# First loads of an attention and expert kernel spread over two queues in another order, with the function table loaded between them

## The chip, the core and the metric

The kernel runs on one core of a Trainium2 chip. The metric is the device time of one execution in microseconds. Five engines work side by side, each through its own list of instructions in order: PE (TensorE: matrix products, with weight loads shown apart as PEld), DVE (VectorE), ACT (ScalarE), POOL (GpSimd) and SP (SyncE). DMAs are issued by instructions on SP and ACT here, and each of the two feeds a queue of its own; an instruction that issues a DMA stands in its engine's list like any other.

## What is computed

The reference, cut to what matters:

```
scores = scale * np.matmul(q, k.transpose(0, 1, 3, 2))        # q, k, v: (2, 8, 576, 64)
kth = np.partition(scores, -top_k, axis=-1)[..., -top_k:-top_k + 1]     # top_k = 32
scores = np.where(scores >= kth, scores, -1000000000.0)
attn = np.exp(scores - np.max(scores, axis=-1, keepdims=True))
attn = attn / (np.sum(attn, axis=-1, keepdims=True) + 1e-09)
attn_out = np.matmul(attn, v)
...
x = _moe_ref(x, ...)       # each row to its one best of 8 experts, limited capacity
return _moe2_ref(x, ...)   # the same without a limit
```

In an expert layer a row goes through `relu(x @ w1[e]) @ w2[e]` and is scaled by its gate weight.

## The kernel before, in words

Attention comes first. The two batches of eight heads are cut into eight units of two heads, and each unit has nine tiles of 128 query rows (four for each head, and one that holds the last 64 rows of both), so 72 tiles. For a tile PE makes the scores of 128 rows against 576 keys, ACT copies them out of PE's accumulators (L478), DVE finds the 32 largest of each row with a chain of folds, maxima and replacements (L505 to L525), POOL and ACT form what lies below the limit (L597, L594), PE turns that (L603, L604), ACT takes the exponential and PE multiplies with v (L624). The two expert layers follow.

The opening is written by hand in `attention()` and in `begin()`. A product with full accuracy is had by splitting k and q into a rounded part and a rest: `part_of` has ACT write the rounded part (L712), DVE subtract it (L717) and POOL copy k (L714). `whole` has PE turn the parts (L285) so that the head's 64 numbers lie on partitions, and ACT or DVE copies them out (L723, L725). `scores(0, 0)` follows once the last 64 rows have been turned too (`put_tails`, L299).

Ahead of `begin()` stand the first instructions of three lists. PE has 17 products of constants into `xb` (`spin`, L124), which keep it at work until data come. SP and ACT issue the loads of unit 0: `load(0, ("k",))` on SP (L261 the first 512 rows of both heads in one DMA of 256 KB, L262 the last 64 rows, 32 KB) and `load(0, ("q",), nc.scalar)` on ACT (L259 twice, 128 KB for each head, and L262). ACT then loads its function table for the exponential (L796) by a small activation `warm`. SP goes on with q of unit 1, v of unit 0 (`vraw`, L253 and L254), k of unit 1, the gate weights and the rest. ACT's next instruction after `warm` is L712 on the first head of k.

Each DMA of SP and ACT adds to a semaphore when it has landed, and there are eight such semaphores, DMAHW0 to DMAHW7, which the build deals out in turn to these DMAs. A DMA that is given a semaphore already dealt out carries a wait for that semaphore's earlier DMA, and the wait stands in the list of the engine that issues it.

Of the kernel before, what the change touches and what calls it, by code (L numbers as in the profile page):

```python
# [10 lines left out]
F32 = mybir.dt.float32  # L11
# [4 lines left out]
AF = mybir.ActivationFunctionType  # L16
# [38 lines left out]
def attn_moe_moe_kernel(ctx, tc, q, k, v, g1, w11, w12, capacity, g2, w21, w22, out):  # L55
    nc = tc.nc
    B, H, S, D = q.shape
# [4 lines left out]
    NC = (S + 127) // 128  # L62
    TAIL = S - (NC - 1) * 128
# [7 lines left out]
    with tc.manual_schedule():  # L71
# [12 lines left out]
        coef = consts.tile([128, 3], F32)  # L84
# [107 lines left out]
    def attention():  # L192
# [4 lines left out]
        M = NC - 1  # L197
# [4 lines left out]
        with tc.tile_pool(name="ald", bufs=2) as ld, tc.tile_pool(name="awk", bufs=2) as wk, \  # L202
                tc.tile_pool(name="aps", bufs=1, space=PS) as ps, tc.manual_schedule():
            st = {}
            held_t = []
            for i in range(2):
                qt = wk.tile([128, 2, 192], F32R, name=f"qtail{i}", bufs=1)
                nc.gpsimd.memset(qt.bitcast(F32), 0.0)
                xl = wk.tile([128, NC, 2, XW], F32, name=f"xl{i}", bufs=1)
                vT = wk.tile([128, NC, 128], F32, name=f"vT{i}", bufs=1)  # L210
# [3 lines left out]
            shifted, under, vx = [], [], []  # L214
# [18 lines left out]
            xo = xb[:, :6 * XW].rearrange("p (g h w) -> p g h w", h=2, w=XW)  # L233
            zero = blank
            pend = []

            def load(u, what=("k", "q", "v"), eng=None):
                b, p = divmod(u, HP)
                z = st.setdefault(u, {"vT": held_t[u % 2][0], "xl": held_t[u % 2][1], "qtail": held_t[u % 2][2],
                                      "v": vx[u % 4]})  # L240
                dma = (eng or nc.sync).dma_start
                for nm in what:
                    s_ = {"k": k, "q": q, "v": v, "w": v}[nm][b, 2 * p:2 * p + 2]
                    if nm == "v":
                        if "vw" not in z:
                            load(u, ("w",))
                        for hh in range(2):
                            dma(z["v"][:, :M, hh, :D], s_[hh, :M * 128, :].rearrange("(s c) d -> s c d", s=128))
                        dma(z["v"][:TAIL, M, :, :D], s_[:, M * 128:, :].rearrange("h s d -> s h d"))
                    elif nm == "w":  # L250
                        t = z["vw"] = ld.tile([128, NC, 2, D], F32, name="vraw", bufs=2)
                        for hh in range(2):
                            dma(t[:, :M, hh], s_[hh, :M * 128, :].rearrange("(s c) d -> s c d", s=128))  # L253
                        dma(t[:TAIL, M], s_[:, M * 128:, :].rearrange("h s d -> s h d"))  # L254
                    else:
                        t = ld.tile([128, 2, NC, D], F32, name=nm + "raw", bufs=2)
                        if nm == "q":
                            for hh in range(2):
                                dma(t[:, hh, :M], s_[hh, :M * 128, :].rearrange("(c s) d -> s c d", s=128))  # L259
                        else:  # L260
                            dma(t[:, :, :M], s_[:, :M * 128, :].rearrange("h (s c) d -> s h c d", s=128))  # L261
                        dma(t[:TAIL, :, M], s_[:, M * 128:, :].rearrange("h s d -> s h d"))  # L262
                        z[nm] = t.rearrange("s h c d -> s c h d")
# [426 lines left out]
            def spin(n, o):  # L690
                for _ in range(n):
                    idle_product(o)
# [97 lines left out]
            seq = [(u, t) for u in range(NU) for t in order[u]]  # L790
            pairs = {}
            spin(17, xb[:, :256])
            load(0, ("k",))
            load(0, ("q",), nc.scalar)
            warm = wk.tile([128, 1], F32, name="warm", bufs=1)
            nc.scalar.activation(warm, coef[:, :1], AF.Exp)  # L796
            load(1, ("q",))
            load(0, ("w",))
            load(1, ("k",))
# [120 lines left out]
            for i in range(L - 4):  # L920
                k_, j_ = divmod(i, 2)
# [81 lines left out]
            z = st[u]  # L1003
# [13 lines left out]
            for c in range(NC):  # L1017
                w, k_ = c % 2, c // 2
# [1088 lines left out]
    rank_cuts = (0, 3, 6, 9, None)  # L2107
    w2_order = ((0, 1), (2, 3), (4, 5), (6, 7), (0, 1), (2,), (3, 4, 5, 6, 7))
    repair(attention())
    small = [ctx.enter_context(tc.tile_pool(name=f"msm{i}", bufs=1)) for i in range(2)]  # L2110
    onehot = small[0].tile([128, 128 * max(B * NC, NCOL + nov[0])], BF, name="onehot")
# [37 lines left out]
```

## Time and profile before

| what | value |
|---|---|
| median of 3 runs | 582.66 us (582.62 to 582.76) |
| the profiled execution, its own time | 583.19 us |
| its span, first to last instruction | 581.5 us |
| share of PE, DVE, ACT, POOL busy | 97%, 82%, 72%, 46% |
| mean granted clock of TensorE | 0.996 |

A busy share is time in which the engine had an instruction under way, whatever that instruction was worth: PE's spins count too. The profiled execution took 1.69 us more than its span, which lies outside the first and last instruction, and 0.53 us more than the median.

### The profile page before, as it was taken

How to read it: one execution, taken by the hardware profiler on the slowest of the kernel's cores; microseconds unless marked ns; L12 is line 12 of the kernel's file. 1: busy time of each engine (PE TensorE's matmuls, PEld its weight loads, DVE VectorE, ACT ScalarE, POOL GpSimd, SP SyncE). 2: the span in 40 equal slices, each digit the busy share in tenths (PEclk: the TensorE clock that was granted, in tenths of full speed). 3: DMA queues.
4: the chain of work that ended last, by engine and by line, in shares of the span. 5: the costliest groups of instructions: out<-in, count | busy, mean ns of one | idle time of the engine just before them, and what ended most of it. 6: DMA issues, size and time to landing. Idle time of an engine off the chain costs nothing. (4 is left out here: it accounts for less than half of the span.)

```text
span 581.5 us, 13994 instructions
## 1 busy us (share of the span) xinstructions
PE 566.0 (97%) x4786; PEld 539.2 (93%) x4786; DVE 475.5 (82%) x1588; ACT 419.4 (72%) x1040; POOL 267.1 (46%) x600
## 2 busy tenths in 40 slices
PE   8999999999999999989999999999999999999994
PEld 6799999999999999889999999998998899999993
DVE  6999999999999999868788788552588788889640
ACT  6789998999898988637687787452465677878550
POOL 8768888988898798546320111010103302220010
PEclk9999999999999999999999999999999999999998
DMA  6630513161211482055998767875777767678650
GB/s 145 143 83 2 169 46 114 45 127 43 70 48 62 70 254 77 23 196 181 349 280 282 221 227 250 287 236 198 237 253 244 278 232 260 225 249 298 211 203 14
DMA packets 85200, 100.76 MB, mean 173 GB/s; under 512 B 33957, under 2 KB 46757, under 8 KB 85120
## 3 DMA queue, kind: packets, MB, share of 16 engines
q1 hardware_dynamic: 79136, 86.69, 48.2%
q0 software_dynamic: 3728, 10.70, 5.4%
q10 hardware_dynamic: 2256, 2.39, 1.3%
q8 instruction: 40, 0.66, 0.5%
q14 instruction: 40, 0.33, 0.2%
HBM read 86.51 MB, written 13.74 MB: 172 GB/s over the span
## 5 line engine op out<-in xcount | busy, mean ns | idle before, releaser
L624 PE MATMUL xb<-vx,pT 128*128 128x73 f32 (+1 forms) x800 | 94.0, 266 | 0.2 <-ACT pT L1014 0.2
L1367 PE MATMUL pp<-xT,w1c 128*128 128x352 f32 (+4 forms) x316 | 92.4, 361 | 0.4 <-DVE xT L1323 0.4
L1288 DVE TENSOR_TENSOR w2c<-raw,w2c 128x512 fp32r<-128x512 f32 x112 | 74.5, 684 | 18.6 <-ACT w2c L1287 16.8
L624 PEld LDWEIGHTS xb<-vx,pT 128*128 128x128 f32 (+1 forms) x800 | 87.1, 181 | 2.5 <-issue 1.3
L1406 PE MATMUL pp<-hT,w2c 128*128 128x416 f32 (+4 forms) x320 | 88.7, 356 | 0.1
L1408 PE MATMUL pp<-hT,w2c 128*128 128x208 f32 (+4 forms) x320 | 77.8, 243 | 0.0
L1369 PE MATMUL pp<-xT,w1c 128*128 128x176 f32 (+4 forms) x316 | 77.0, 244 | 0.0
L1287 ACT ACTIVATE w2c<-raw 128x512 fp32r<-128x512 f32 x112 | 67.4, 624 | 8.7 <-PE pp L1408 3.7
L603 PE MATMUL pt<-ident,shifted 128*128 128x128 f32 x350 | 67.5, 278 | 0.0
L604 PE MATMUL pt<-negid,under 128*128 128x128 bf16 x350 | 63.5, 219 | 0.5 <-ACT under L594 0.5
L1288 DVE TENSOR_TENSOR w1c<-raw,w1c 128x512 fp32r<-128x512 f32 x88 | 55.9, 684 | 9.5 <-ACT w1c L1287 7.5
L1339 ACT ACTIVATE t<-pp 128x208 f32<-128x208 f32 (+4 forms) x120 | 37.6, 314 | 34.2 <-PE pp L1369 21.6
L1408 PEld LDWEIGHTS pp<-hT,w2c 128*128 128x128 f32 x320 | 61.0, 191 | 0.0
L1406 PEld LDWEIGHTS pp<-hT,w2c 128*128 128x128 f32 x320 | 60.0, 187 | 1.0 <-DVE hT L1333 0.8
L1367 PEld LDWEIGHTS pp<-xT,w1c 128*128 128x128 f32 x316 | 59.4, 188 | 1.4 <-DVE xT L1323 0.8
L1369 PEld LDWEIGHTS pp<-xT,w1c 128*128 128x128 f32 x316 | 60.4, 191 | 0.0
L1469 POOL DMA_INDIRECT out_dram<-yr,sidx x14 | 13.6, 972 | 101.1 <-ACT yr L1450 84.7
L594 ACT ACTIVATE under<-s,nb 128x576 bf16<-128x576 f32 x70 | 54.9, 786 | 1.5 <-POOL nb L586 1.3
L1792 POOL DMA_DIRECT2D y<-yr x13 | 7.6, 582 | 105.3 <-issue 45.1
L523 DVE MAX8 top<-ypair 128x8 f32<-128x160 f32 x192 | 54.7, 313 | 0.0
L597 POOL TENSOR_SCALAR shifted<-s,nb 128x576 f32<-128x576 f32 x70 | 52.3, 747 | 3.9
L603 PEld LDWEIGHTS pt<-ident,shifted 128*128 128x128 f32 x350 | 49.2, 140 | 3.6
(421 smaller groups left out, 1547.8 us busy)
## 6 DMA issues: line engine op xcount, KB each, us to landing
raw<-in_moe_w_dram SPq DMA_DIRECT2D x60, 1024.0 KB, 5.1
w1c<-in_moe_w_dram SPq DMA_DIRECT2D x8, 512.0 KB, 6.3
y<-blank SPq DMA_DIRECT2D x3, 769.5 KB
out_dram<-blank SPq DMA_DIRECT2D x3, 768.0 KB
y<-yr POOLq DMA_DIRECT2D x8, 256.5 KB
kraw<-in_k_dram SPq DMA_DIRECT2D x8, 256.0 KB, 3.4
vraw<-in_v_dram SPq DMA_DIRECT2D x16, 128.0 KB, 2.8
vx<-in_v_dram SPq DMA_DIRECT2D x16, 128.0 KB, 2.8
```

Of the source, the lines that this page charges most:

```text
L523: ops.append(lambda w=w, cur=cur: nc.vector.max(w, cur))
L594: nc.scalar.activation(under[k % 3][:, :S], s, AF.Relu, bias=nb[:, 1:2], scale=-BIG)
L597: nc.gpsimd.tensor_scalar(shifted[k % 3][:, :S], s, nb[:, 0:1], 1.0, op0=OP.add, op1=OP.mult)
L603: both = (nc.tensor.matmul(pt[:, o], shifted[k % 3][:, o], ident, is_transpose=True, start=True, stop=False), nc.tensor.matmul(pt[:, o], u ...
L604: nc.tensor.matmul(pt[:, o], under[k % 3][:, o], negid, start=False, stop=True))
L624: nc.tensor.matmul(o, pT[:, c2, cols], z["v"][:, c2, hh], start=(c2 == 0), stop=(c2 == NC - 1))
L1287: nc.scalar.activation(o[:, 0], src_, AF.Copy)
L1288: nc.vector.tensor_tensor(o[:, 1], src_, o[:, 0].bitcast(F32), op=OP.subtract)
L1367: nc.tensor.matmul(ph[:, :2 * n].rearrange("p (w n) -> p w n", w=2), w[f][:, 0, d], xT[:, d, :, :n], start=st, stop=False)
L1369: nc.tensor.matmul(ph[:, :n], w[f][:, 1, d], xT[:, d, 0, :n], start=False, stop=sp)
L1406: nc.tensor.matmul(py[:, :2 * n].rearrange("p (w n) -> p w n", w=2), w[f][:, 0, o], hT[:, f, :, :n], start=st, stop=False)
L1408: nc.tensor.matmul(py[:, :n], w[f][:, 1, o], hT[:, f, 0, :n], start=False, stop=sp)
```

## The change

Unit 0's k and q are now loaded by a function of their own, `load_first`. ACT issues one DMA (the last 64 rows of k), loads its function table and runs `warm`, and then issues a second DMA (the second head of q). SP issues k's first 512 rows, the first head of q and the last 64 rows of q. The same five DMAs move the same bytes into tiles of the same names and sizes; nothing behind them in the program is edited.

```diff
+            def load_first(then):
...
+                kt = ld.tile([128, 2, NC, D], F32, name="kraw", bufs=2)
+                qt = ld.tile([128, 2, NC, D], F32, name="qraw", bufs=2)
+                head = lambda hh: (qt[:, hh, :M], q_[hh, :M * 128, :].rearrange("(c s) d -> s c d", s=128))
+                tail = lambda t, s_: (t[:TAIL, :, M], s_[:, M * 128:, :].rearrange("h s d -> s h d"))
+                nc.sync.dma_start(kt[:, :, :M], k_[:, :M * 128, :].rearrange("h (s c) d -> s h c d", s=128))
+                nc.scalar.dma_start(*tail(kt, k_))
+                nc.sync.dma_start(*head(0))
+                then()
+                nc.sync.dma_start(*tail(qt, q_))
+                nc.scalar.dma_start(*head(1))
...
             spin(17, xb[:, :256])
-            load(0, ("k",))
-            load(0, ("q",), nc.scalar)
             warm = wk.tile([128, 1], F32, name="warm", bufs=1)
-            nc.scalar.activation(warm, coef[:, :1], AF.Exp)
+
+            def table_load():
+                nc.scalar.activation(warm, coef[:, :1], AF.Exp)
+
+            load_first(table_load)
             load(1, ("q",))
```

Lines behind the new function are 16 and then 18 higher than before. What the built programs hold at three places, with the semaphores that each instruction waits for:

The first place is the start of ACT's list. `kraw` and `qraw` are the loaded tiles, 128x4x64 is one head's first 512 rows, 64x2x64 the last 64 rows of both heads; `ks` and `qs` are the split parts. Before, and then now:

```order
L259 DMA qraw<-in_q_dram 128x4x64 x2
L262 DMA qraw<-in_q_dram 64x2x64
L796 ACT_TABLE_LOAD
L796 ACTIVATE warm<-coef 128x1 [waits DVE_49]
L712 ACTIVATE ks<-kraw 128x4x64 [waits DMAHW1_49]
L712 ACTIVATE qs<-qraw 128x4x64 [waits DMAHW0_49]
L712 ACTIVATE ks<-kraw 64x2x64 [waits DMAHW3_49]
L712 ACTIVATE qs<-qraw 64x2x64 [waits DMAHW5_49]
```

```order
L246 DMA kraw<-in_k_dram 64x2x64
L812 ACT_TABLE_LOAD
L812 ACTIVATE warm<-coef 128x1 [waits DVE_49]
L250 DMA qraw<-in_q_dram 128x4x64 [waits DMAHW7_49]
L728 ACTIVATE ks<-kraw 128x4x64 [waits DMAHW1_49]
L728 ACTIVATE qs<-qraw 128x4x64 [waits DMAHW2_49]
L728 ACTIVATE ks<-kraw 64x2x64 [waits DMAHW0_49]
L728 ACTIVATE qs<-qraw 64x2x64 [waits DMAHW3_49]
```

Two of the three DMAs have left the list, one of another tile has come in front, and the DMA of q's second head now stands between `warm` and the first split, with a wait for DMAHW7.

The second place is the start of SP's list; `vraw` is v of unit 0, and the two L259 (now L275) load q of unit 1. Before, and then now:

```order
L261 DMA kraw<-in_k_dram 128x2x256
L262 DMA kraw<-in_k_dram 64x2x64
L259 DMA qraw<-in_q_dram 128x4x64 x2
L262 DMA qraw<-in_q_dram 64x2x64
L253 DMA vraw<-in_v_dram 128x4x64 [waits DMAHW0_49]
L253 DMA vraw<-in_v_dram 128x4x64 [waits DMAHW1_49]
L254 DMA vraw<-in_v_dram 64x2x64 [waits DMAHW2_49]
```

```order
L245 DMA kraw<-in_k_dram 128x2x256
L247 DMA qraw<-in_q_dram 128x4x64
L249 DMA qraw<-in_q_dram 64x2x64
L275 DMA qraw<-in_q_dram 128x4x64 x2
L278 DMA qraw<-in_q_dram 64x2x64
L269 DMA vraw<-in_v_dram 128x4x64
L269 DMA vraw<-in_v_dram 128x4x64 [waits DMAHW0_49]
L270 DMA vraw<-in_v_dram 64x2x64 [waits DMAHW1_49]
```

SP has one DMA more ahead of v, and the first half of v is now issued without a wait; the second half waits for DMAHW0, where before the first half did.

The third place is PE's list where v of unit 0 is turned (L776 before, L792 now). Before, and then now:

```order
L285 MATMUL pg<-identr,ks 128x128 [waits Activation_49,Pool_49]
L285 MATMUL pg<-identr,ks 128x128 x3
L776 MATMUL pt<-ident,vraw 128x128 [waits DMAHW1_49,DMAHW0_49,Activation_49]
L776 MATMUL pt<-ident,vraw 128x128 x3
L776 MATMUL pt<-ident,vraw 128x64 [waits DMAHW2_49]
```

```order
L301 MATMUL pg<-identr,ks 128x128 [waits Activation_49,Pool_49]
L301 MATMUL pg<-identr,ks 128x128 x3
L792 MATMUL pt<-ident,vraw 128x128 [waits DMAHW7_49,DMAHW0_49,Activation_49]
L792 MATMUL pt<-ident,vraw 128x128 x3
L792 MATMUL pt<-ident,vraw 128x64 [waits DMAHW1_49]
```

The products stand where they stood; the two halves of v, which signalled DMAHW0 and DMAHW1, now signal DMAHW7 and DMAHW0.

## Rows read from the trace of the kernel before

**Rows 1.** The page's head and its busy shares.

```profile
span 581.5 us, 13994 instructions
PE 566.0 (97%) x4786; PEld 539.2 (93%) x4786; DVE 475.5 (82%) x1588; ACT 419.4 (72%) x1040; POOL 267.1 (46%) x600
```

**Rows 2.** Windows: stretch, us, busy per engine (instructions), granted clock, DMA share, GB/s.

```profile
10.00:15.00 5.00, 4.10 (x29) 2.93 (x28) 4.99 (x22) 3.78 (x11) 4.42 (x9) 1.00 0.64 142
...
40.00:100.00 60.00, 60.00 (x585) 58.01 (x584) 59.67 (x238) 54.64 (x137) 49.15 (x98) 1.00 0.31 90
100.00:230.00 130.00, 129.46 (x1260) 124.74 (x1259) 129.72 (x527) 115.85 (x284) 113.81 (x288) 1.00 0.36 89
```

**Rows 3.** Timeline of DVE: start, us, operation, [idle before it <- what ended it].

```profile
4.54 0.43 DVE L717 TENSOR_TENSOR ks<-kraw,ks 128x256 fp32r<-128x256 f32 x1 [1.58 <-ACT ks L712]
...
9.60 0.31 DVE L505 TENSOR_TENSOR hi<-sc,s 128x144 f32<-128x144 f32 x1 [0.46 <-ACT s L478]
```

**Rows 4.** Timeline of ACT from its start; ACTq rows are DMAs it issues.

```profile
0.85 1.07 ACTq L259 DMA_DIRECT2D qraw<-in_q_dram  x2
1.96 0.72 ACTq L262 DMA_DIRECT2D qraw<-in_q_dram  x1
2.71 1.28 ACT L796 ACT_TABLE_LOAD   x1 [2.71 <-issue]
4.00 0.20 ACT L796 ACTIVATE warm<-coef 128x1 f32<-128x1 f32 x1
4.11 0.40 ACT L712 ACTIVATE ks<-kraw 128x256 fp32r<-128x256 f32 x1
```

**Rows 5.** Timeline of PE from its start.

```profile
1.25 3.79 PE L124 MATMUL xb<-idle,ones 128*128 128x256 bf16 x17 [1.25 <-DVE idle L75]
5.02 0.75 PE L285 MATMUL sc<-identr,ks 128*128 128x128 f32 x4
...
6.60 0.60 PE L124 MATMUL sc<-idle,ones 128*128 128x512 bf16 x2
...
7.73 0.82 PE L124 MATMUL sc<-idle,ones 128*128 128x512 bf16 x3
8.27 0.54 PE L473 MATMUL pt<-qkT 128*128 128x288 f32 x2
```

**Rows 6.** Line L124 up to 5.1 us: durations min/median/max, first and last start.

```profile
L124 PE MATMUL xb<-idle,ones x17: 372/421/421, 1.2 to 4.6; 128*128 128x256 bf16 x17
```

**Rows 7.** Timeline of SP's queue from its start.

```profile
0.86 0.44 SPq L261 DMA_DIRECT2D kraw<-in_k_dram  x1
1.36 0.75 SPq L262 DMA_DIRECT2D kraw<-in_k_dram  x1
2.15 1.34 SPq L259 DMA_DIRECT2D qraw<-in_q_dram  x2
3.53 0.62 SPq L262 DMA_DIRECT2D qraw<-in_q_dram  x1
4.46 1.25 SPq L253 DMA_DIRECT2D vraw<-in_v_dram  x2
```

**Rows 8.** Waits of SP's queue up to 40 us: total us, times, longest.

```profile
SPq L253 <- DMA qraw<-in_q_dram: 0.3, 1, 0.3
```

**Rows 9.** Tile vraw, whole span: time of its loads from issue to landing.

```profile
DMA to landing us min/median/max: 2.4/2.8/3.2
```

**Rows 10.** Tile qraw, first 12 us: the same of its loads there.

```profile
DMA to landing us min/median/max: 3.9/3.9/3.9
```

**Rows 11.** Windows behind the last product; columns as in the second group.

```profile
574.00:574.50 0.50, 0.04 (x1) 0.00 (x0) 0.00 (x0) 0.43 (x1) 0.00 (x0) 1.00 0.00 0
576.00:576.50 0.50, 0.00 (x0) 0.00 (x0) 0.00 (x0) 0.00 (x0) 0.01 (x1) 1.00 0.00 0
576.50:577.00 0.50, 0.00 (x0) 0.00 (x0) 0.00 (x0) 0.00 (x0) 0.00 (x0) 0.58 0.74 287
```

**Rows 12.** Waits of PE, whole span: the longest.

```profile
PE pp L1859 <- ACTq L1661: 1.5, 1, 1.5
```

More of the change, by code (lines that the diff above doesn't have):

```diff
@@ L235, in attention @@
             pend = []
+            def load_first(then):
+                z = st.setdefault(0, {"vT": held_t[0][0], "xl": held_t[0][1], "qtail": held_t[0][2], "v": vx[0]})
+                k_, q_ = k[0, :2], q[0, :2]
+                kt = ld.tile([128, 2, NC, D], F32, name="kraw", bufs=2)
[8 more added lines that the diff above has]
+                nc.scalar.dma_start(*head(1))
+                z["k"], z["q"] = (t.rearrange("s h c d -> s c h d") for t in (kt, qt))
             def load(u, what=("k", "q", "v"), eng=None):
```

## Prediction

> **What bounds the kernel now.** I read the page's head first: PE is busy 97% of a span of 581.5 us [rows 1]. That is no proof that PE is the bound, since it is also fed with products of constants. The windows tell more: from 10 us to 230 us DVE is busy 4.99 of 5.00, 59.67 of 60 and 129.72 of 130 us [rows 2]. Through the whole attention DVE has no gap in which a delay could vanish, and it enters this stretch with one instruction, the fold L505 at 9.60, which waits for ACT's first copy of scores [rows 3]. So the time from the launch to this fold goes into the total one to one, and everything that the change touches lies ahead of it.
>
> The timelines of the opening show what decides 9.60. ACT issues three DMAs to 2.68, loads its table from 2.71, runs `warm` at 4.00 and starts the split of k's first head at 4.11, with no idle time named before it [rows 4]: k had landed by then, and ACT's list is what was late. DVE subtracts at 4.54 because ACT got there [rows 3], PE turns at 5.02, and the first scores begin at 8.27 [rows 5]. From ACT's first split to DVE's first fold are 9.60 - 4.11 = 5.49 us of a chain in which each engine waits for the other.
>
> **The change, part by part.** The sum is made against the profiled execution, 583.19 us, which lies 0.53 above the median of the runs; I take that off at the end.
>
> *k's main DMA* stays SP's first, at 0.86 [rows 7]: nothing.
>
> *The other four loads.* SP gets two of q for one of k's, so it issues five DMAs between k and v's first half where it issued four. Those four took from 1.36 to 3.53 + 0.62 = 4.15 [rows 7]. One more of 128 KB takes half of 1.34, so 0.67, on SP, or half of 1.07, so 0.53, on ACT [rows 4, 7]; with the gaps between issues v's first half is issued at about 4.8 (4.6 to 4.9), where before it stood at 4.46. k's tail, q's first head and q's tail are under way long before ACT comes to use them (below), so I cost their new places at nothing; the cover is the hold of the next part, and without it a late first head of q would show at once.
>
> *The function table.* ACT's list now has one small DMA ahead of it (0.72 for this shape [rows 4]), so the table load begins near 1.6 instead of 2.71 and `warm` is through near 3.1. By itself that frees ACT 1.1 us earlier, less one DMA issue.
>
> *The wait that comes with it.* Behind `warm` stands the DMA of q's second head, and in the built program it waits for DMAHW7. Seven of the eight semaphores belong to loads issued before it or beside it; PE's turning of v waits for 7 and 0, and 0 is the one for which SP's second half of v waits itself. So 7 is signalled by the **first half of v**, SP's seventh DMA. That such a wait holds the issuing engine, and not the transfer alone, has its row: in the kernel before, SP's first v load waited for the semaphore of ACT's q load, and SP stood still for 0.3 us [rows 8], from 4.15 to 4.46 [rows 7]. Queued behind the waiting DMA on ACT are all four splits of unit 0; DVE waits for them, PE for DVE.
>
> Its length: v's first half is issued near 4.8 and must land. Loads of this kind took 2.4 to 3.2 us, median 2.8 [rows 9]; q of unit 1, which went out in the crowd of the opening with 288 KB on ACT's queue beside it, took 3.9 [rows 10]. ACT's queue now carries only 32 KB at that time, so I take 2.8, and keep 2.4 and 3.9 as the ends. v lands at 4.8 + 2.8 = 7.6; ACT issues its DMA in 0.53 and splits k at 8.15 instead of 4.11: **+4.0 us** (4.6 + 2.4 + 0.53 gives +3.4; 4.9 + 3.9 + 0.53 gives +5.2).
>
> The Trainium skill, "DMA: Bandwidth & Descriptors", section "Anatomy of one DMA", gives a fixed 2.0 us and bytes at 436 GB/s for a DMA of the gpsimd path; as an estimate from that page 128 KB would need 2.3 us and the hold would cost 3.5. No load of this shape in the trace is that quick, so the measured 2.8 stands.
>
> *TensorE's clock.* PE's 17 spins start 0.21 us apart for 256 columns (4.6 - 1.2 over 16 steps [rows 6]), which is the 1.2 GHz level; the spins of 512 columns from 6.60 on are 0.22 apart (0.82 for three against 0.60 for two [rows 5]), which is 2.4 GHz. So in the kernel before the clock doubled between, at about 6.5, with PE at work without a break since 1.25. Now PE stands idle from the last spin, near 4.8, to the first turning at 5.02 + 4.0 = 9.0. At the kernel's end, the last product is over at 574.04, the granted clock is still 1.00 in the half microsecond from 576.0 and 0.58 in the next [rows 11]: it fell some 2.5 us after the work did. I therefore expect the work at 9.0 to meet the low level. Its price: between nothing (the clock comes back as soon after 9.0 as it did after 5.02, 1.5 us) and a full new start of 6.5 - 1.25 = 5.3 us, which is 3.8 us more at half speed, at most 1.9 us lost if PE were the bound all through. On the way to the first scores it mostly is: five spins of 512 columns stand between (five times 0.21 more), with the turnings and scores to be slowed as well. I take **+1.0 us**, the middle.
>
> The Trainium skill, "TensorE: Matmul & The Clock Gate", part 1, calls the low level the default, which activity releases; by that page the term would go towards its upper end, 1.9, and the sum to 588.6 (a rival below). The row of the kernel's end agrees on the fall, and no row before shows how soon work brings the clock back after a break, so I keep the middle.
>
> *q's second head* goes out at 7.6 and lands 2.8 to 3.9 later, by 11.5. It is needed only after the first scores, which move from 8.27 to about 13. Covered by 1.5 us; without that cover the second head's split would be what is late next.
>
> **The sum.** 583.19 + 4.0 + 1.0 = 588.2 for a profiled execution; less 0.53 it is **587.7 us** against the median of 582.66. Both low ends give 582.66 + 3.4 = 586.1, both high ends 582.66 + 5.2 + 1.9 = 589.8.
>
> **The rivals.**
>
> *The clock does not matter* (held or given back at once): 582.66 + 4.0 = 586.7. For it: the fall at the end took 2.5 us, and PE idles 4; against it: that is already longer.
>
> *The clock starts anew in full*, 5.3 us at the low level with PE as the bound: 582.66 + 4.0 + 1.9 = 588.6. For it: the launch took that long with PE at work all the time. Against it: between first turning and first fold PE also waits for ACT and DVE, and such waits do not grow with PE's clock. This is what the page on TensorE would have it be.
>
> *v lands as soon as in a quiet stretch*, or sooner, as the page on DMA would have it: 3.5 + 1.0, so 587.2. For it: ACT's queue is emptier than before. Against it: SP alone still has 830 KB ahead of v's last byte.
>
> *Not slower: ACT is not held.* The place is ACT's DMA behind `warm`, reached near 3.1. If its wait were met by then, ACT would split k as soon as k has landed, up to 0.5 us sooner than 4.11. The price on the path is smaller: PE's last spin starts at 4.6 [rows 6] and is over 0.21 later, so the turning could begin near 4.83 instead of 5.02, a gain of 0.2 us at most, 582.5. It decides at v's landing: the time stays within 0.2% of now (1.17 us, about what a measurement of this kernel can tell from no change) only if ACT's split starts before 5.3, so v lands before 4.7, when SP has hardly issued it. The rows speak against it; what remains is that the wait stands for another load than I read.
>
> *The delay is absorbed.* Some later wait for a thing that does not move would have to be as long as the delay. PE's longest is 1.5 us [rows 12], and DVE has no gap to 230 us [rows 2]. Up to 1.5 would give 586.2 and still be slower.
>
> **How the numbers follow.** The forecast as it stands, 0.50. Clock without effect, 0.14; clock anew in full, 0.12; v early, 0.11; part of it absorbed, 0.07: all slower by over 0.2%, together 0.94. ACT not held, 0.06: 0.05 no change, 0.01 faster (a gain over 1.17 us has no row that could give it). The range of 585.8 to 589.5 takes in the rivals that are slower and nearly both joint ends of the two terms.
>
> **What would show it.** In the profile of the changed kernel: the table load begins near 1.6; ACT then stands idle between `warm` and the DMA of q's second head for some 4.5 us, ended by the DMA of `vraw`; the first split at 8.15; PE idle from 4.8 to 9.0; spins of 512 columns 0.43 apart for a while after 9.0 if the clock fell, 0.22 if not; DVE's first fold at 14.6 instead of 9.60 and no gap from there on. I am wrong if ACT's first split starts before 5.3, if v lands outside 7.0 to 8.8, or if DVE's fold is late as said and the end is not.

## The result, and the profile after

The changed kernel takes **587.97 us**, the median of 4 runs (587.82 to 589.8). The kernel before took 582.64 in the 4 runs beside it (582.37 to 582.76). The ratio is 1.0099, with a 95% interval of 1.0087 to 1.0111: the change makes the kernel 5.33 us slower. The execution whose profile is read here took 587.82, with a span of 586.2.

ACT's timeline answers to [rows 4] (start, us, operation, [idle before it <- what ended it]):

```profile
0.86 0.71 ACTq L246 DMA_DIRECT2D kraw<-in_k_dram  x1
1.61 1.28 ACT L812 ACT_TABLE_LOAD   x1 [1.61 <-PEq L2150]
2.90 0.20 ACT L812 ACTIVATE warm<-coef 128x1 f32<-128x1 f32 x1
7.16 0.44 ACTq L250 DMA_DIRECT2D qraw<-in_q_dram  x1
7.64 0.42 ACT L728 ACTIVATE ks<-kraw 128x256 fp32r<-128x256 f32 x1 [4.54 <-DMA vraw<-in_v_dram]
```

The table load is early, as the change says: it begins at 1.61 instead of 2.71, and `warm` is through at 3.10. Then ACT has nothing until the DMA of q's second head at 7.16. The idle time in front of the first split is put down to a load of v, a tile that no split reads. k had long landed (issued at 0.87, its loads took at most 3.3 us); the split comes 3.53 us later than before (7.64 against 4.11).

SP's timeline answers to [rows 7], and the tile `vraw` up to 12 us to [rows 9]:

```profile
2.67 1.14 SPq L275 DMA_DIRECT2D qraw<-in_q_dram  x2
3.85 0.63 SPq L278 DMA_DIRECT2D qraw<-in_q_dram  x1
4.52 1.28 SPq L269 DMA_DIRECT2D vraw<-in_v_dram  x2
```

```profile
DMA to landing us min/median/max: 2.4/2.6/2.8
```

4.52 and the median of 2.6 make 7.12. That is the moment at which ACT moves on.

PE's timeline answers to [rows 5], and DVE's to [rows 3]:

```profile
1.25 3.73 PE L124 MATMUL xb<-idle,ones 128*128 128x256 bf16 x17 [1.25 <-DVE idle L75]
8.57 0.75 PE L301 MATMUL sc<-identr,ks 128*128 128x128 f32 x4 [3.59 <-DVE ks L733]
...
10.14 1.08 PE L124 MATMUL sc<-idle,ones 128*128 128x512 bf16 x2
...
12.02 1.46 PE L124 MATMUL sc<-idle,ones 128*128 128x512 bf16 x3
12.92 1.04 PE L489 MATMUL pt<-qkT 128*128 128x288 f32 x2
```

```profile
8.09 0.42 DVE L733 TENSOR_TENSOR ks<-kraw,ks 128x256 fp32r<-128x256 f32 x1 [5.13 <-DMA vraw<-in_v_dram]
...
14.93 0.31 DVE L521 TENSOR_TENSOR hi<-sc,s 128x144 f32<-128x144 f32 x1 [1.36 <-ACT s L494]
```

PE stands 3.59 us idle between the spins and the first turning. Behind that the same operations are slower than in [rows 5]: two spins of 512 columns take 1.08 instead of 0.60 and three take 1.46 instead of 0.82, and ACT's copy of the scores comes so late that the fold waits 1.36 instead of 0.46. The windows show why (stretch, us, busy per engine with instructions, granted clock, DMA share, GB/s):

```profile
8.00:10.00 2.00, 1.43 (x11) 1.43 (x12) 1.65 (x5) 1.36 (x5) 1.18 (x3) 0.55 0.93 217
10.00:15.00 5.00, 4.98 (x20) 3.10 (x20) 1.35 (x3) 2.21 (x6) 3.93 (x8) 0.50 0.65 139
15.00:20.00 5.00, 4.17 (x31) 3.03 (x29) 4.84 (x21) 3.69 (x10) 4.36 (x11) 1.00 0.66 158
45.00:105.00 60.00, 60.00 (x585) 58.04 (x583) 59.68 (x240) 54.56 (x136) 48.77 (x98) 1.00 0.31 91
105.00:235.00 130.00, 129.53 (x1260) 124.84 (x1259) 129.76 (x526) 115.73 (x285) 113.53 (x289) 1.00 0.36 89
```

The granted clock is 0.50, the 1.2 GHz level, from soon after 8 us to 15 us, so all the work up to the first fold runs at it. From 15 us it is full. The trace's own record of the granted clock begins at 4.79 with full speed, falls to half at 8.21 and returns at 15.03. (Ahead of the first entry of that record the windows read 1.00 whatever the clock was: the spins up to 4.6 ran 0.21 us apart, which is the 1.2 GHz level.) DVE then has no gap, as in [rows 2], and the delay stays: the fold is 5.33 us late (14.93 against 9.60), and a top-8 late in the attention stands at 232.52 in the changed kernel (first line below) and at 227.20 in the kernel before (second), 5.32 later.

```profile
232.52 0.53 DVE L539 MAX8 top<-ypair 128x8 f32<-128x160 f32 x2
```

```profile
227.20 0.54 DVE L523 MAX8 top<-ypair 128x8 f32<-128x160 f32 x2
```

So the 5.33 us are 3.53 of hold and 1.80 behind it, on the way from the first split to the fold: 14.93 - 7.64 = 7.29 us where it was 5.49. At the last product of the two profiled executions the difference is 4.63. It is still 5.15 at 450 us and is 4.63 by 480 us; four of the runs below show a step of 0.5 to 0.6 at the same place against this profile of before, so it belongs to that one execution, which was 0.53 above its median. The medians agree with the fold.

### The profile page after: what moved, and what is told of

It reads as the page before. It is cut to its first block, busy times and chain, and to the rows that moved or that the text cites. A ratio compares the mean times of both kernels' runs of the same rounds, so it can differ in the third digit from the quotient of the medians.

```text
span 586.2 us, 13994 instructions
## 1 busy us (share of the span) xinstructions
PE 567.6 (97%) x4786; PEld 540.5 (92%) x4786; DVE 475.8 (81%) x1588; ACT 419.4 (72%) x1040; POOL 266.4 (45%) x600
## 4 chain that ended last, share of the span: by engine, by line
PE 40%; DMA 8%; issue 5%; DVE 1%; POOLq 0%; POOL 0%; ACT 0%; DVEq 0%; ACTq 0%
PE pp L1385 8%; DMA out_dram<-yr,sidx 8%; PE pp L1424 7%; PE pp L1387 4%; PE pp L1371 3%; PE pp L1426 3%; PE pt L1335 2%; PE pl L1438 2%; PE pp L1418 1%; PE pt L1475 1%; PE pp L1877 1%; PE pp L1420 1%; PE pp L1422 1%; PE pp L1421 1%; PE pp L1374 1%
```

## The experiments

All times are set against the runs of the kernel before that stood beside them: 582.66 for the first four below, 582.78 for the next four, 583.15 for the last. "Fold" is DVE's first fold, 9.60 before and 14.93 after.

| run | first split | fold | time | over before | ratio, 95% interval |
|---|---|---|---|---|---|
| q's second head ahead of the table | 4.05 | 9.87 | 582.39 | -0.27 | 0.9989 to 1.0006 |
| q's second head on SP | 3.75 | 9.37 | 582.77 | +0.11 | 0.9998 to 1.0018 |
| after, 44 spins | 7.79 | 13.03 | 590.52 | +7.86 | 1.0121 to 1.015 |
| before, 1 spin | 4.11 | 11.41 | 586.74 | +4.08 | 1.0049 to 1.0078 |
| after, spins of 512 columns | 7.73 | 13.39 | 585.86 | +3.08 | 1.0039 to 1.0067 |
| before, spins of 16 columns | 4.12 | 11.27 | 584.89 | +2.11 | 1.0024 to 1.0054 |
| before, 44 mixed spins | 4.17 | 9.85 | 587.89 | +5.11 | 1.0069 to 1.0097 |
| gate weights seventh | 7.15 | 14.64 | 587.69 | +4.91 | 1.0067 to 1.0095 |
| k of unit 1 seventh | 7.89 | 15.27 | 589.11 | +5.96 | 1.0086 to 1.012 |

My theory had two parts: ACT's list is held by a DMA that must wait for the semaphore it shares with SP's seventh DMA, and the clock is at its low level when work comes again, since PE idles through the hold. The rival to the first was that something else of the new order is slow; the rival to the second that the 1.80 us behind the hold are not the clock.

**Taking the hold away, in two ways.** First the second head of q goes ahead of the table load:

```diff
                 nc.scalar.dma_start(*tail(kt, k_))
+                nc.scalar.dma_start(*head(1))
                 nc.sync.dma_start(*head(0))
                 then()
                 nc.sync.dma_start(*tail(qt, q_))
-                nc.scalar.dma_start(*head(1))
```

> The changed kernel with both of ACT's DMAs ahead of the function table: SP's order and the tiles stay, ACT has no DMA with a wait left. If the hold (and the clock that it costs) is the whole loss, ACT's first split starts at 3.5 to 3.7, DVE's first fold at 9.4 to 9.7, and the time is 582.4 to 582.9, level with the kernel before. If the new order of the loads costs something by itself (q's first head or unit 1 late), the fold is at 10 or later and the time 583.5 or more.

Then it stays in its place and is issued by SP:

```diff
-                nc.scalar.dma_start(*head(1))
+                nc.sync.dma_start(*head(1))
```

> The changed kernel with q's second head issued by SP behind q's tail: ACT issues k's tail, loads its table at 1.6 as in the changed kernel, and has no held DMA. If the hold is the loss: ACT's first split at 3.4 to 3.7, 582.3 to 582.9. If loading the table early or the order on SP is what costs, the time stays above 584.

With nothing else changed both are level with the kernel before: 582.39 and 582.77, and both intervals hold 1. ACT's timeline of the run with SP:

```profile
1.61 1.28 ACT L812 ACT_TABLE_LOAD   x1 [1.61 <-PEq L2150]
2.91 0.20 ACT L812 ACTIVATE warm<-coef 128x1 f32<-128x1 f32 x1
3.75 0.42 ACT L728 ACTIVATE ks<-kraw 128x256 fp32r<-128x256 f32 x1 [0.64 <-DMA kraw<-in_k_dram]
```

The table is as early as in the changed kernel, and now ACT waits 0.64 for k itself, which is the load that the split reads. So the early table buys 0.36 us at the split (3.75 against 4.11) and 0.23 at the fold (9.37 against 9.60), and no more, because k's landing is next in line. That gain is too small to be seen in the time. As far as the intervals tell, moving the loads is harmless to the time; the one DMA behind the table costs everything. In the first of the two ACT waits for the loads that it does read, k's and q's first head:

```profile
4.05 0.42 ACT L728 ACTIVATE ks<-kraw 128x256 fp32r<-128x256 f32 x1 [0.30 <-DMA kraw<-in_k_dram]
4.79 0.42 ACT L728 ACTIVATE qs<-qraw 128x256 fp32r<-128x256 f32 x1 [0.32 <-DMA qraw<-in_q_dram]
```

Its split missed the 3.5 to 3.7 that I gave (with SP it was 3.75, 0.05 above my upper end), and its fold came at 9.87, 0.27 late. The interval of the time reaches up to +0.35 and can't tell this from nothing.

**Which DMA ACT waits for.** The semaphore is the point of the theory: the wait should follow whatever SP issues seventh, v or not. In one run the loads of the gate weights (16 KB) stand there, in the other the 256 KB part of k of unit 1:

```diff
             load(1, ("q",))
-            load(0, ("w",))
-            load(1, ("k",))
             for i, g in enumerate((g1, g2)):
                 nc.sync.dma_start(wg[:, i], g.rearrange("(c p) e -> p c e", p=128))
+            load(0, ("w",))
+            load(1, ("k",))
```

> The changed kernel with the two 16 KB loads of the gate weights issued on SP ahead of the four of v and of k of the second unit, so that SP's seventh DMA is a gate load. Theory (ScalarE's DMA of q's second head waits for whatever the seventh DMA of SP is, for the semaphore that both share, and needs nothing of v): the wait of the first split is put down to the load of wg and no longer to v; issued at 4.5, landed 2.4 to 2.7 later, split at 7.4 to 7.8, time 587.3 to 588.0. Rival (it waits for v itself, or for a number of bytes on the queue): the wait stays with v, which is now issued at about 5.6, split at 8.6 or later, time 588.8 to 590.

```diff
             load(1, ("q",))
-            load(0, ("w",))
             load(1, ("k",))
+            load(0, ("w",))
```

> The changed kernel with the load of k of the second unit (its main part 256 KB, its tail 32 KB) issued on SP ahead of v, so that SP's seventh DMA is the 256 KB part. Theory (ScalarE's DMA waits for SP's seventh DMA whatever it is): the wait of the first split is put down to a load of k; issued at 4.5, landed 2.9 to 3.4 later, split at 7.9 to 8.5 instead of 7.64, first fold 0.2 to 0.9 later than in the changed kernel, time 588.1 to 588.9. Rival (it waits for v, which is now issued at about 5.8): the wait stays with v, split at 8.7 or later, time 589 or more.

The first splits of the two runs, the gate weights first:

```profile
7.15 0.42 ACT L728 ACTIVATE ks<-kraw 128x256 fp32r<-128x256 f32 x1 [4.04 <-DMA wg<-in_moe_w_gate_dram]
```

```profile
7.89 0.42 ACT L728 ACTIVATE ks<-kraw 128x256 fp32r<-128x256 f32 x1 [4.79 <-DMA kraw<-in_k_dram]
```

The name behind the wait changes with the seventh load, and v, issued later in both, is no longer named. The split moves with the landing: 7.15, 7.64 and 7.89 for a gate load, v and k; the fold follows with 14.64, 14.93 and 15.27, and the time with +4.91, +5.33 and +5.96. (With the gate weights the split was 0.25 earlier than I had set as the lower end, with k at the lower end itself. The first time lies inside what I gave, the second 0.21 above it.) ACT needs nothing of these loads. What the three have in common is the place in SP's list, and with it the semaphore that the built program names at ACT's DMA.

The Trainium skill, "DMA: Bandwidth & Descriptors", section "Why a DMA increments its semaphore by 16 and not by 1", says that with two DMAs in flight on one semaphore a count can be reached before the first has fully landed, and asks for one semaphore per transfer in flight. The built program holds to that at this place: it puts a wait in front of the second issue, and these runs show what that costs when the issuing engine has other work behind it (3.53 us at the split).

**The clock, first try: more or fewer spins.** To keep PE busy through the hold I gave the changed kernel 44 spins instead of 17; to have the clock low without a hold I gave the kernel before 1.

```diff
-            spin(17, xb[:, :256])
+            spin(44, xb[:, :256])
```

> The changed kernel with 44 spins instead of 17, so that PE has work through the hold (27 more at 0.11 to 0.21 us, to about 8.5). The hold stays: ACT's first split at 7.6. If the clock is the second part of the loss, DVE's first fold comes at 13.0 to 13.5 instead of 14.93 and the time is 586.0 to 586.6, some 1.6 below the changed kernel. If the clock does not matter, 588.0 and the fold at 14.9.

```diff
-            spin(17, xb[:, :256])
+            spin(1, xb[:, :256])
```

> The kernel before with 1 spin instead of 17, so that PE is idle up to its first turning at 5.0 and nothing is held. If the clock has its price without any hold: spins of 512 columns 0.43 apart behind 5.0, first fold 0.8 to 2.0 later than 9.60, time 583.4 to 584.7. If the clock does not matter: 582.7.

Both times are misses (586.0 to 586.6 and 583.4 to 584.7 were expected), yet both openings did as the clock theory said. With 44 spins the fold came at 13.03, 1.90 earlier than in the changed kernel at nearly the same split; with 1 spin the fold of the kernel before came at 11.41, 1.81 late. Each then lost time far from the opening, near 260 us, where attention goes over to the experts. PE's timeline there, with 44 spins:

```profile
263.49 0.61 PE L1877 MATMUL pp<-w2c,w1c 128*128 128x128 f32 x4
267.36 1.86 PE L1877 MATMUL pp<-w2c,w1c 128*128 128x128 f32 x7 [3.27 <-issue]
```

and PE's longest wait with 1 spin, 250 to 275 us (us in all, times, longest):

```profile
PE pp L1859 <- PEq L1661: 3.9, 1, 3.9
```

In the kernel before the longest there is 1.5 [rows 12]. "issue" is time for which the profile shows nothing that PE waits for, and PEq is PE's own sequencer. What the two runs share is that PE has 54 instructions more, or 32 fewer (a spin is a weight load and a product), so that everything behind stands at another place of its list. As tests of the clock by the time they were spoiled.

**The clock, second try: as many spins, of another width.**

```diff
-            spin(17, xb[:, :256])
+            spin(17, xb)
```

> The changed kernel with its 17 idle products at the start made 512 columns wide instead of 256, so that TensorE works until about 7 us and the number of its instructions stays the same (the earlier run with 44 idle products had more of them, and lost 4.8 us at 255 to 267 us, where TensorE stood at 'issue'). Theory (the hold of ScalarE costs 3.5 us, the clock that falls at 8.2 another 1.8): first split of k still at 7.6 to 7.8, clock full through the first turns, first fold at 12.9 to 13.3 instead of 14.93, no new stand at 255 to 267, time 585.9 to 586.6. Rival (the surplus over the hold isn't the clock, or what the clock gives comes back later): first fold at 14.6 or later, or time 587.6 to 588.2.

```diff
-            spin(17, xb[:, :256])
+            spin(17, xb[:, :16])
```

> The kernel before with its 17 idle products 16 columns wide instead of 256: TensorE goes idle at 2 to 3 us, with no change in the number of instructions and with all loads as before. Theory (the clock alone costs 1.8 in the first turns; the 2.3 us that the kernel before with one idle product lost at 255 to 267 us came from the number of TensorE's instructions): first fold at 11.2 to 11.6 instead of 9.60, clock low until some 13 us, time 584.2 to 584.8. Rival 1 (the loss at 255 to 267 hangs on the late opening, not on the number): the same fold, time 586.4 to 587.0. Rival 2 (no cost of the clock here): 582.4 to 583.0.

PE's timeline of the changed kernel with wide spins, then DVE's fold:

```profile
1.25 5.69 PE L124 MATMUL xb<-idle,ones 128*128 128x512 bf16 x17 [1.25 <-DVE idle L75]
8.72 0.53 PE L301 MATMUL sc<-identr,ks 128*128 128x128 f32 x4 [1.78 <-DVE ks L733]
...
10.03 0.61 PE L124 MATMUL sc<-idle,ones 128*128 128x512 bf16 x2
```

```profile
11.99 1.47 DVE L733 TENSOR_TENSOR ks<-kraw,ks 128x256 fp32r<-128x256 f32 x1 [1.41 <-ACT ks L728]
13.39 0.29 DVE L521 TENSOR_TENSOR hi<-sc,s 128x144 f32<-128x144 f32 x1
```

PE of the kernel before with narrow spins:

```profile
1.25 0.60 PE L124 MATMUL xb<-idle,ones 128*128 128x16 bf16 x17 [1.25 <-DVE idle L75]
5.03 0.75 PE L285 MATMUL sc<-identr,ks 128*128 128x128 f32 x4 [3.18 <-DVE ks L717]
...
6.76 1.01 PE L124 MATMUL sc<-idle,ones 128*128 128x512 bf16 x2
...
8.57 1.46 PE L124 MATMUL sc<-idle,ones 128*128 128x512 bf16 x3
```

The two run in opposite directions and agree. With wide spins PE idles 1.78 instead of 3.59, two spins of 512 columns take 0.61 and not 1.08, and with the hold in full (split at 7.73) the time is only 3.08 over before. With narrow spins no load and no split has moved (4.12), PE idles 3.18, the same spins take 1.01 and 1.46, the fold comes 1.67 late and the time is 2.11 over before. In this run the clock did not fall, it had not risen: the record of the granted clock begins only at 10.32. Neither run has a stand of more than 1.1 us on PE near 260 us.

The top-8 that stood at 227.20 and, in the changed kernel, at 232.52 stands here with wide spins (first line) and with narrow ones (second):

```profile
230.63 0.53 DVE L539 MAX8 top<-ypair 128x8 f32<-128x160 f32 x2
```

```profile
229.26 0.53 DVE L523 MAX8 top<-ypair 128x8 f32<-128x160 f32 x2
```

That is 3.43 and 2.06 late, together 5.49 where the changed kernel is 5.32 late. By the medians it is 3.08 with the hold and 2.11 with the low clock, together 5.19 where the change costs 5.33. In the two spoiled runs the same top-8 stands at 230.60 (44 spins) and 229.31 (1 spin), so up to the end of the attention they say the same. The sums agree better than their parts are known: the intervals leave the first median between 2.3 and 3.9 and the second between 1.4 and 3.2. Nor is the first the hold quite alone, since its first turnings ran at the full level (1.31 us from 8.72 to the spins at 10.03) where the kernel before took 1.58.

Whether the clock had risen before the hold made little difference. With k of unit 1 seventh the record of full speed begins at 5.61, after the spins were over at 5.03, and ends at 9.03; with the gate weights it begins only at 13.76. Behind the split these two lost 1.89 and 2.00 us, where the changed kernel lost 1.80.

Some details missed by a little. The fold with wide spins came at 13.39, just past the 13.3 that I gave: in the profiled execution DVE's subtract of k took 1.47 us, against 0.72 in the changed kernel, for a reason that I did not look for; this execution took 586.45, 0.59 above the median of its runs, and the median, 585.86, is 0.04 below the range. The time with narrow spins, 584.89, is 0.09 above its range, and the clock was back at 10.32 and not at some 13.

**The number of instructions by itself.** The kernel before with 44 spins that end when its 17 did:

```diff
-            spin(17, xb[:, :256])
+            spin(14, xb[:, :256])
+            spin(30, xb[:, :16])
```

> The kernel before with 14 idle products of 256 columns and 30 of 16 columns, which together end about when the 17 did (5 us): 27 more pairs of TensorE's instructions, as in the run with 44 idle products, and the opening otherwise the same. Theory (the number of instructions alone moves a stand of TensorE at 255 to 267 us): first fold at 9.5 to 9.9, then a loss of 2 to 5 us at 255 to 267 with a wait of 3 to 4 us at 'issue' or at TensorE's own sequencer, time 584.7 to 587.7. Rival (the number is nothing, the loss came with the later or slower opening): no new wait there, time 582.4 to 583.0.

PE's timeline near 260 us, and two windows there:

```profile
260.42 0.61 PE L1860 MATMUL pp<-w2c,w1c 128*128 128x128 f32 x4
264.30 2.08 PE L1860 MATMUL pp<-w2c,w1c 128*128 128x128 f32 x8 [3.27 <-issue]
```

```profile
261.20:264.20 3.00, 0.00 (x0) 0.00 (x0) 1.42 (x3) 0.79 (x2) 2.48 (x6) 0.71 0.68 179
264.30:269.30 5.00, 5.00 (x23) 5.00 (x24) 1.07 (x2) 0.54 (x2) 2.78 (x3) 0.50 0.98 357
```

The opening is the old one (split 4.17, fold 9.85), and still 5.11 us are lost, a little over the 2 to 5 that I had given (the time is 0.19 above its range): PE stands 3.27 us, the same as in the changed kernel with 44 spins, at the same instruction of the same line. Then it works 5 us at the low level: the clock fell during the stand (0.71 as a mean over it, 0.50 behind). So the surplus of the run with 44 spins came with the number of PE's instructions and not with the opening. For the run with 1 spin the narrow spins say the same: their opening is as late (fold 11.27 against 11.41), their number is 17, and the stand is missing. What PE waits for in such a stand is not settled by these runs: the program has a branch there for the rare case of an expert with too many tokens (L1661 lies in it), but what it has to do with the stand no run here shows.

## Why the prediction was right, step by step

- **A late fold goes one to one into the time.** Right: fold +5.33, medians +5.33, and 5.32 still there at 232 us. That the first two are equal to the hundredth is chance; in the runs with wide and narrow spins the fold and the later top-8 differ by 0.4 (3.79 and 3.43, 1.67 and 2.06).
- **The other four loads at nothing, under the cover of the hold.** Right, and so is the warning behind it: in the two runs without a hold ACT waits for q's first head, 0.32 and 0.29 us.
- **The table load near 1.6, `warm` through near 3.1.** 1.61 and 3.10.
- **The wait stands for SP's seventh DMA.** Right for its name, and the two runs with another seventh load show that it is the place in the list that counts.
- **The size of the hold, 4.0.** Mis-sized: 3.53, inside its ends of 3.4 to 5.2. v was issued at 4.52 and not at 4.8 (the end I gave was 4.6), because q's first head took 0.47 to issue where I had reckoned 0.67, and the two heads of unit 1 behind it 1.14 where they had taken 1.34 [rows 7]; it landed after about 2.6 and not 2.8, and ACT's issue took 0.44 and not 0.53. The estimate of 3.5 that I gave from the Trainium skill, "DMA: Bandwidth & Descriptors", section "Anatomy of one DMA", is the nearer one, though its landing of 2.3 is still too short for the 2.6 seen: the early issue makes up for it.
- **The clock, +1.0.** Mis-sized, and this is the step that failed by most: 1.80 in the profile, and 1.67 at the fold, 2.06 at the late top-8 and 2.11 in the time of the run in which the clock is late and nothing else, against my upper end of 1.9. I took the middle because no row of before shows how soon the clock returns. It returned at about 15 us, when PE had worked since 8.57 with hardly a break, so the whole way to the fold was at the low level: the rival "the clock starts anew in full" describes what happened. Its upper end was no bound, though: the low stretch behind 8.57 lasted 6.5 us, where I had taken the 5.3 of the launch. With PE as the bound all the way to the fold that would come to some 2.4 (an estimate: half of the 6.4 from 8.57 to 14.93 less the 1.5 of before), so the 1.80 also says that PE isn't the bound throughout. The Trainium skill, "TensorE: Matmul & The Clock Gate", part 1, calls the low level the default that activity releases; the runs agree (with narrow spins, PE idle until 5.03, two spins of 512 columns took 1.01 where they took 0.60), and its side was the better one.
- **The sum.** 3.53 + 1.80 = 5.33 in place of 4.0 + 1.0 = 5.0. The two errors, 0.5 and 0.8, have opposite signs, so that 587.7 is nearer to 587.97 than either term deserved. That much of it is luck.
- **q's second head is covered.** It was issued at 7.16 and needed at most 3.2 to land, so it was there by 10.4, and the split of the second head of k, which comes ahead of its own, began at 12.41.
- **ACT not held.** Fell: the split stood at 7.64, and 5.3 would have been needed. What that rival would have gained at best, 0.2 at the turning, the run with SP measured as 0.33 there (4.69 against 5.02) and 0.23 at the fold.

## What to carry to other kernels

A DMA that stands in the list of a computing engine is an instruction like any other: whatever it waits for, the work behind it waits for too (here 3.53 us at the split). Where more DMAs are in flight than there are semaphores for them, read in the built program whose semaphore each late one shares, and leave such an issue to a queue that has nothing else to do; here one word (SP instead of ACT) was worth 5.2 us. The stand of TensorE early in this kernel was paid twice, once in itself and once at the low clock behind it (3.53 and 1.80 us). An experiment on this should keep the number of TensorE's instructions and change only their width.

## What I had not expected of the hardware

- **TensorE can lose 3 to 4 us far away from an edit.** 27 more spins at the start, and nothing else of weight, cost 3.27 us of standing near 261 to 264 us and 5 us at half clock behind it; 16 fewer left 3.9 us at the product right behind the branch. With 17 spins of any width the longest wait there was 1.1 to 1.5 us.
- **The clock outlasts the work, by times that differ.** In the changed kernel PE's spins were over at 4.98 and the clock fell at 8.21, 3.2 us later (the mean of 0.55 over 8 to 10 us agrees: 0.2 us at 1.00 and 1.8 at 0.50). At the old end of the kernel it was 2.5 us [rows 11]. In the stand of the last experiment it fell at 262.47, 1.4 us after the last product, with another wait of 1.09 us shortly before. A gap of 1.78 us, with wide spins, did no harm, but that is what one profile shows and no safe length.
